# Two more and six more warm-up matmuls in the waits for the first batch's input

## The chip, the cores and the metric

The kernel runs on one core of one Trainium2 chip. The metric is the device time of the kernel in microseconds (us); lower is better. A core has five engines that work in parallel: PE (TensorE, matmuls; its weight loads are listed as PEld), DVE (VectorE), ACT (ScalarE), POOL (GpSimd) and SP (SyncE, here only the issuer of transfers). The "span" is the time from the first to the last instruction of a profiled execution; the measured time is mostly 2.1 us longer.

## The reference

For each of 8 batches, `x` (3008 x 256) goes through a Fourier transform along its length, a product with a complex filter, and the inverse transform. The result, 24064 tokens of width 256, goes through an MLP with 2048 hidden units.

```python
X = np.fft.rfft(x, axis=1)
F = (filt_r + 1j * filt_i)[None, :, :]
y = np.fft.irfft(X * F, n=x.shape[1], axis=1)
h = y.reshape(B * S, D) @ w_in
g = h * (1.0 / (1.0 + np.exp(-beta * h)))
out = g @ w_out
```

## The kernel before

The transforms are done as matmuls with tables of sines and cosines. Batch 0 has nothing to hide behind: the MLP can't start before it is transformed, so its first 40 us are a start-up stage. In it x arrives in chunks, PE multiplies eight "groups" of x by a table (`first1`), ACT or DVE copies each result from PSUM to SBUF (an "eviction"), PE transposes the results (`turn_a`), and `product` multiplies them by the filter on DVE. Meanwhile DVE, POOL and ACT compute the tables.

Matmuls on a tile of zeros, whose result nobody reads, fill PE's waits in order to keep its clock up:

```python
    def warm(n, cols=512):
        for _ in range(n):
            nc.tensor.matmul(pw[0][:, :cols], lhsT=wz[:, :P], rhs=wz[:, :cols], start=True, stop=True)
    ...
    X_FIRST = [(0, 80, 0, JG), (80, NP, 0, JG), (0, 80, JG, 2 * JG), (80, NP, JG, J)]   # the x chunks, in order
    X_FIRST += [(0, 80, g * JG, (g + 1) * JG) for g in range(2, NJG)]
    ...
    nc.sync.dma_start(mark[:], x_cur[:1, JG, :])     # SP's later filter loads wait for the third chunk
    ...
    warm(12)
    ...
    angles(0, nc.vector)      # half of the angles of table t2 on DVE
    angles(1, gp)             # the other half on POOL
    ...
    for i in range(2):
        first1(i, (True, True))                      # evictions: True is ACT, False is DVE
        warm(2)
    t2_part(0, 0)
    first1(2, (False, False))
    warm(2)
    for part in (1, 2):
        t2_part(0, part)
    for go in load_filter(fri, filt_i, M, *FG[2], nc.scalar):
        go()
    for i in range(3, 5):
        first1(i, (False, False))
        warm(2)
    t2_more(0, nc.vector)                            # three copies inside table t2, on DVE
    first1(5, (True, True))
    warm(2)
    first1(6, (True, True))
    warm(2)
    first1(7, (False, True))
    ...
    # product(i): reads the filter tile fri
        for dst, ps in zip((p_t, q_t), pss):
            nc.vector.tensor_tensor(dst[:], ps[:], fri[:, 2 * i : 2 * i + 2, :], ALU.mult)
    ...
    nc.vector.tensor_scalar_mul(t3[M:P], t3b[M:P], -1.0)   # the negation, at the start of the MLP
```

The first filter part is issued by POOL, behind x, on the software queue (q0). The other parts are issued by SP (queue q1) and ACT (q10), which are hardware queues.

## Time and profile before

Three runs: 790.11, 790.13 and 791.49 us, median 790.13 us.

| What | Before |
|---|---|
| PE busy over the span | 98% |
| Longest PE wait in start-up | 2.28 us, ending at 10.21 us |
| PE clock at half | from 11.6 to 15.0 us |
| First transpose of batch 0 (PE) | 17.09 us |
| First product of batch 0 (DVE) | 19.70 us |
| First MLP matmul (PE) | 41.36 us |

The page of the kernel before says what bounds the whole: busy time by engine, and the chain of waits by line. Lines 826 and 791 are the two MLP matmuls.

```profile
PE 772.1 (98%) x6001; PEld 548.0 (69%) x6097; DVE 395.7 (50%) x643; ACT 596.9 (75%) x920; POOL 144.6 (18%) x143
...
PE 92%; DVE 3%; issue 2%; POOL 2%; ACT 1%; DVEq 0%; ACTq 0%; POOLq 0%
```

The MLP can't be moved by a few warm-ups. Only an earlier start of it can count. PE's timeline of the kernel before shows the start-up. The columns are start, duration, engine, source line, operation, output and input, count, and in brackets the idle time before it with what ended that. `pw` is a warm-up, `psa` a group of x, `pb` the first transposes.

```profile
1.18 4.53 PE L186 MATMUL pw<-wz 128*128 128x512 bf16 x12 [1.18 <-DVE wz L181]
6.22 0.50 PE L347 MATMUL psa<-t1b,xg 94*128 94x96 bf16 x8 [0.51 <-DMA xg<-in_x_dram]
...
7.33 0.60 PE L186 MATMUL pw<-wz 128*128 128x512 bf16 x2
10.21 0.50 PE L347 MATMUL psa<-t1b,xg 94*128 94x96 bf16 x8 [2.28 <-DMA xg<-in_x_dram]
...
12.53 1.05 PE L186 MATMUL pw<-wz 128*128 128x512 bf16 x2
13.38 0.84 PE L347 MATMUL psa<-t1b,xg 94*128 94x96 bf16 x8
...
15.73 0.51 PE L347 MATMUL psa<-t1b,xg 94*128 94x96 bf16 x8
17.09 0.83 PE L409 MATMUL pb<-ident,a_t 128*128 128x128 bf16 x12 [0.86 <-POOL tiny L308]
```

The wait of 2.28 us is what the change aims at. Later a pair of warm-ups takes 1.05 us instead of 0.60, and a group 0.84 instead of 0.50. The table of windows of the same kernel shows the cause. Its columns are the stretch, its length, PE's busy time and instructions, the granted clock (1.00 is full), the DMA engines' busy share, and GB/s.

```profile
11.50:12.00 0.50, 0.46 (x3) 0.62 1.19 307
12.00:13.00 1.00, 1.00 (x11) 0.50 0.97 228
...
15.00:16.00 1.00, 1.00 (x18) 0.98 1.45 335
```

The clock is at half for 3.4 us. But is PE what the next stage waits for? The timeline of DVE and POOL in the same trace says otherwise. Lines 289 to 291 are the three table copies, 269 and 270 POOL's angle operations, the last `a_t<-psa` is the eviction that the first transpose needs.

```profile
10.58 2.89 DVE L107 CAST a_t<-psa 128x384 bf16<-128x384 f32 x6 [1.75 <-PE psa L347]
11.61 2.81 POOL L269 TENSOR_SCALAR r<-u 128x768 f32<-128x768 f32 x1
13.38 0.35 DVE L289 TENSOR_SCALAR t<-t 128x768 bf16<-128x768 bf16 x1
13.65 0.98 DVE L290 COPY t<-t 128x768 bf16<-128x768 bf16 x1
14.50 1.81 POOL L270 TENSOR_TENSOR u<-u,r 128x768 f32<-128x768 f32 x1
14.55 1.97 DVE L291 COPY t<-t 128x768 bf16<-128x768 bf16 x1
16.45 0.54 DVE L107 CAST a_t<-psa 128x384 bf16<-128x384 f32 x1
...
19.70 0.69 DVE L442 TENSOR_TENSOR pb_t<-ps,fri 128x512 bf16<-128x512 f32 x1 [1.52 <-DMA fri<-in_filt_i_dram]
```

The second copy ends at 14.63 us, just after POOL's line 269 (14.42 us); the third ends at 16.52 us, just after line 270 (16.31 us). Only then does DVE evict, and the transpose follows at 17.09 us. The label "POOL tiny" on that transpose is an inference of the profile; the eviction that ended at 16.99 us fits better. The first product then waits 1.52 us for its filter.

### The profile page before, as it was taken

To read this page: it belongs to the slowest core of one execution; us is meant where nothing else is said; L and a number is where in the kernel's file an instruction comes from. 1 tells how busy PE (TensorE), PEld (TensorE's weight loads), DVE (VectorE), ACT (ScalarE), POOL (GpSimd) and SP (SyncE) were. 2 spreads that over 40 slices of the span, in tenths; PEclk is the share of its full clock that TensorE was granted. 3 is DMA by queue.
4 is the path that set the end of the run, shared out by engine and by line. 5 is a ranking of instruction groups with operands and counts; after the bars stand their busy time and mean duration, and the time that the engine had idled before them with its cause. 6 is when DMAs were issued, how large, how long until landed. Compare 5 with 4: busy or idle time off the path is not lost.

```text
span 790.8 us, 15274 instructions
## 1 busy us (share of the span) xinstructions
PE 772.1 (98%) x6001; PEld 548.0 (69%) x6097; DVE 395.7 (50%) x643; ACT 596.9 (75%) x920; POOL 144.6 (18%) x143
## 2 busy tenths in 40 slices
PE   7899999999999999999999999999999999999998
PEld 4767667766677667776668766687667766776665
DVE  7946935755527464465634746367462760500101
ACT  5887886886678866788667876778767788677776
POOL 8421510430014200131002310024100340000000
PEclk9999999999999999999999999999999999999999
DMA  8978678116811178011860229402370214010101
GB/s 183 235 191 215 145 207 224 56 67 187 204 56 47 68 200 218 29 68 60 216 190 28 78 103 197 155 30 92 126 208 27 74 68 127 28 54 27 55 27 53
DMA packets 83379, 91.43 MB, mean 116 GB/s; under 512 B 3758, under 2 KB 73536, under 8 KB 82286
## 3 DMA queue, kind: packets, MB, share of 16 engines
q1 hardware_dynamic: 79756, 73.16, 30.0%
q0 software_dynamic: 2816, 16.26, 10.8%
q10 hardware_dynamic: 736, 1.05, 0.6%
q8 instruction: 47, 0.77, 0.4%
q14 instruction: 24, 0.20, 0.1%
HBM read 57.16 MB, written 46.66 MB: 131 GB/s over the span
## 4 chain that ended last, share of the span: by engine, by line
PE 92%; DVE 3%; issue 2%; POOL 2%; ACT 1%; DVEq 0%; ACTq 0%; POOLq 0%
PE acc L826 42%; PE hps L791 37%; PE ps L599 3%; PE ps L522 3%; PE ps L621 2%; PE ps L647 2%; DVE ost L107 1%; POOL xg L116 0%; POOL r L269 0%; DVE qb_t L442 0%; ACT a L105 0%; DVE pb_t L442 0%; PE pb L409 0%; PE psz L452 0%; DVE q_t L636 0%
## 5 line engine op out<-in xcount | busy, mean ns | idle before, releaser
L800 ACT ACTIVATE gT<-hps,beta_sb 128x512 bf16<-128x512 f32 x752 | 516.5, 687 | 175.8 <-PE hps L791 147.9
L826 PE MATMUL acc<-wout_sb,gT 128*128 128x256 bf16 x3008 | 455.1, 272 | 3.8 <-ACT ost L105 0.2
L791 PE MATMUL hps<-y,win_sb 128*128 128x512 bf16 (+7 forms) x1634 | 427.4, 350 | 0.3 <-DVE y L109 0.3
L826 PEld LDWEIGHTS <-gT 128*128 128x128 bf16 x3008 | 285.4, 98 | 132.6 <-issue 4.5
L791 PEld LDWEIGHTS <-win_sb 128*128 128x128 bf16 x1728 | 164.7, 98 | 24.8 <-issue 0.7
L637 POOL TENSOR_TENSOR v_t<-p_t,q_t 128x512 bf16<-128x512 f32 x84 | 106.7, 1270 | 376.3 <-DVE q_t L636 373.7
L107 DVE COPY ost<-acc 128x512 f32<-128x512 f32 (+1 forms) x88 | 56.2, 677 | 193.6 <-PE acc L826 188.0
L107 DVE CAST a<-ps 96x512 bf16<-96x512 f32 x96 | 65.9, 687 | 85.5 <-PE ps L599 85.4
L109 DVE TENSOR_SCALAR y<-ps 128x376 bf16<-128x376 f32 (+2 forms) x120 | 64.5, 541 | 64.4 <-PE ps L522 64.2
L632 DVE TENSOR_TENSOR p_t<-ps,frr 128x512 f32<-128x512 f32 x84 | 58.1, 691 | 31.8 <-PE ps L621 29.5
L636 DVE TENSOR_TENSOR q_t<-ps,fri 64x512 f32<-64x512 f32 x84 | 58.2, 693 | 1.2
L633 DVE SCALAR_TENSOR_TENSOR q_t<-ps,fri 64x512 f32<-64x512 f32 x84 | 57.4, 684 | 1.1
L522 PEld LDWEIGHTS <-zz 96*128 96x128 bf16 x512 | 35.3, 97 | 29.0
L105 ACT ACTIVATE z<-ps 128x512 bf16<-128x512 f32 x84 | 49.5, 589 | 0.7 <-PE ps L647 0.7
L599 PE MATMUL ps<-xg,t 94*96 94x512 bf16 x112 | 41.9, 381 | 0.8
L522 PE MATMUL ps<-t,zz 96*128 96x94 bf16 x448 | 36.7, 204 | 1.1
L116 POOL DMA_DIRECT2D xg<-in_x_dram x22 | 12.1, 556 | 114.3 <-PE acc L826 97.7
L647 PE MATMUL ps<-v_t,t 128*128 128x256 bf16 x168 | 32.1, 273 | 0.4 <-DVE q_t L636 0.4
L621 PE MATMUL ps<-a,t 128*128 128x256 bf16 x168 | 32.1, 273 | 0.4
L621 PEld LDWEIGHTS <-t 128*128 128x128 bf16 x168 | 15.8, 98 | 14.6
L599 PEld LDWEIGHTS <-t 94*96 94x96 bf16 x112 | 13.8, 123 | 12.1
L647 PEld LDWEIGHTS <-t 128*128 128x128 bf16 x168 | 15.4, 98 | 8.1 <-DVE q_t L636 0.9
(118 smaller groups left out, 196.9 us busy)
## 6 DMA issues: line engine op xcount, KB each, us to landing
out_dram<-ost SPq DMA_DIRECT2D x40, 512.0 KB, 2.8
d<-a SPq DMA_DIRECT2D x28, 384.0 KB, 3.5
a<-d SPq DMA_DIRECT2D x28, 384.0 KB, 5.2
d<-z SPq DMA_DIRECT2D x28, 384.0 KB, 2.6
zz<-d SPq DMA_DIRECT2D x28, 384.0 KB, 4.4
xg<-in_x_dram POOLq DMA_DIRECT2D x6, 1280.0 KB, 10.2
frr<-in_filt_r_dram SPq DMA_DIRECT2D x12, 256.0 KB, 6.8
out_dram<-ost SPq DMA_DIRECT2D x22, 128.0 KB, 9.0
```

Of the source, the lines that this page charges most:

```text
L107: nc.vector.tensor_copy(dst, src)
L109: nc.vector.tensor_scalar_mul(dst, src, scale)
L522: nc.tensor.matmul(ps[:, e, :NP], lhsT=zz[:, jj + e, dc * P : (dc + 1) * P], rhs=tab[:], start=True, stop=True,)
L599: nc.tensor.matmul(ps[:KP], lhsT=t1[:], rhs=s["x"][:, 2 * i : 2 * i + 2, :], start=True, stop=True)
L621: nc.tensor.matmul(ps[:, e, :], lhsT=t2[:, k0 + e, 3:5, :].rearrange("p c k -> p (c k)"), rhs=s["a2"][g][:, kk + e, :], start=True, stop=True,
L632: nc.vector.tensor_tensor(p_t[:], ps[:], frr[:, ks_, :], ALU.mult)
L636: nc.vector.tensor_tensor(q_t[:M], ps[M:P], fri[M:P, ks_, :], ALU.mult)
L637: nc.gpsimd.tensor_tensor(v_t[:], p_t[:], q_t[:], ALU.add)
L647: nc.tensor.matmul(ps[:, e, :], lhsT=t3[:, k0 + e, :], rhs=v_t[:, e, :], start=True, stop=True)
L791: nc.tensor.matmul(hps[:, pos - t0 : pos - t0 + ln], lhsT=win_sb[:, dc, fb * P : (fb + 1) * P], rhs=ys[b][:, dc, n0 : n0 + ln], start=(dc ...
L800: nc.scalar.activation(gT[:, :tn], hps[:, :tn], ACT.Silu, scale=beta_sb[:, fb : fb + 1])
L826: nc.tensor.matmul(acc[tb // per][:, tb % per, :], lhsT=gT[:, tb * P : (tb + 1) * P], rhs=wout_sb[:, fb, :], start=(fb == 0 and tb % per = ...
```

## The change

The intent is that PE is never idle for more than a microsecond in the two waits for x, so that the clock does not drop.

```diff
-    warm(12)
+    warm(14)
...
     for i in range(2):
         first1(i, (True, True))
-        warm(2)
+        warm(2 if i == 0 else 8)
     t2_part(0, 0)
```

## The prediction

> **What bounds the kernel now.** From about 41 us on, TensorE: 98% busy over the span, and the chain of waits puts 92% on PE, nearly all in the two MLP matmul lines at a granted clock of 1.00. The change touches only the first 17 us.
>
> **What the change aims at.** In PE's timeline the 12 warm-up matmuls run from 1.18 to 5.71 us; the first x chunk starts at 6.22 us (idle 0.51). After the second group's two warm-ups (7.33 to 7.93 us) PE is idle for 2.28 us until the next x transfer lands (10.21 us). The table of windows shows what follows: clock 1.00 until 11.6 us, 0.50 to about 15.0 us, then 1.00. That stretch of 3.4 us agrees with the window of 3413 ns in the Trainium skill, "TensorE: Matmul & The Clock Gate", Part 1: a window with too much idle halves the clock. In it a warm-up pair takes 1.05 us instead of 0.60, eight 94x96 matmuls 0.84 instead of 0.50.
>
> **Cost.** Warm-ups issue every 0.43 us cold (spacing of their weight loads), 0.22 us warm. Added: 2 in the first wait (0.4 to 0.85 us; the wait holds 0.5) and 6 in the second (1.3 us warm, 2.6 cold; the wait is 2.28). In the traced phase the first wait shrinks to about 0.1 us and the second to about 1.0, no x group is delayed, and I estimate that the throttle goes away. Groups 4 to 7 on PE then finish 1.5 to 2 us earlier (about 14.3 instead of 16.2 us).
>
> **How much is on the critical path: almost nothing.** Three things hide it.
> 1. The evictions of groups 2 to 4 run on DVE back to back from 10.58 to 13.47 us. Then DVE copies the twiddle table: 0.35, 0.98 and 1.97 us, though the same copies take 0.34 to 0.35 us later. They overlap GpSimd's angle operations (11.61 to 14.42, 14.50 to 16.31 us) and end just after them, as in the exclusive shared port pair of the Trainium skill, "SBUF — State Buffer", "Who interferes with whom". The last eviction of group 7 stands behind them and ends at 16.99 us; the first transpose starts at 17.09 us. Neither GpSimd nor DVE waits for PE here.
> 2. Even that start has about 1 us of slack: the first product's PSUM is complete at about 18.62 us, but DVE begins at 19.70 us, idle 1.52 us for the filter transfer, with the DMA engines about full since 4 us.
> 3. From 19.70 to 37.2 us DVE is practically full; only then come the last transposes and the MLP.
>
> So PE finishes the first stage earlier and waits longer for the same events. The gain is 0 in the traced phase; at most some tenths, perhaps 1 us, in runs where the slow stretch overlaps 17 to 20 us. The opposite phase (clock released late, added matmuls cold) delays groups 0 to 2 by 1 to 2 us, also mostly hidden.
>
> **Prediction:** 790.1 us, range 789.3 to 791.3. Faster by over 2%: 0.01; within 2%: 0.98; slower: 0.01.
>
> **What the profile should show.** 36 warm-up matmuls instead of 28; longest PE idle before 17 us about 1 us; the 0.50 stretch gone; group 7 done on PE near 14.3 us, yet the first transpose still at about 17.1 us; first product on DVE near 19.7 us; first MLP matmul near 41.4 us.
>
> **What would make it wrong.** The throttle survives a window about 70% busy; the long DVE copies follow PE or ACT rather than GpSimd; the filter transfer lands earlier, exposing PE; shifted work changes the interleaving later.

## More of the kernel before

One profile was given, with a span of 790.8 us. The execution that it shows took 792.89 us, 1.4 us more than the slowest of the three timed runs.

## The result

A ratio here is the mean time of one kernel's fast runs over the mean of the other's fast runs of the same rounds, so it is not quite the ratio of the medians quoted beside it.

| | Median | Range | Runs |
|---|---|---|---|
| Before (all runs by then) | 791.20 us | 790.11 to 792.99 | 6 |
| After | 791.86 us | 789.49 to 793.27 | 6 |

The ratio is 1.0004, with a 95% interval of 0.9984 to 1.0024: the same. The interval leaves room for a gain of 1.3 us as well as for a loss of 1.9 us. The forecast "within 2%" held. The time did not: 791.86 us lies above the predicted range of 789.3 to 791.3 us.

The profile after has a span of 789.3 us. PE's timeline:

```profile
1.17 4.93 PE L186 MATMUL pw<-wz 128*128 128x512 bf16 x14 [1.17 <-DVE wz L181]
6.22 0.50 PE L347 MATMUL psa<-t1b,xg 94*128 94x96 bf16 x8
...
7.33 1.89 PE L186 MATMUL pw<-wz 128*128 128x512 bf16 x8
9.55 0.50 PE L347 MATMUL psa<-t1b,xg 94*128 94x96 bf16 x8 [0.32 <-DMA xg<-in_x_dram]
...
13.42 0.50 PE L347 MATMUL psa<-t1b,xg 94*128 94x96 bf16 x8
14.45 0.84 PE L409 MATMUL pb<-ident,a_t 128*128 128x128 bf16 x12 [0.53 <-ACT a_t L105]
```

The warm-ups are there, the waits are short, and the table of windows of the kernel after shows the full clock throughout:

```profile
11.50:12.00 0.50, 0.50 (x9) 1.00 1.16 275
12.00:13.00 1.00, 1.00 (x20) 1.00 0.89 208
```

But x also landed earlier, at 9.55 instead of 10.21 us. The change issues no transfer, so this needs another explanation. DVE and POOL in the trace after:

```profile
9.91 2.88 DVE L107 CAST a_t<-psa 128x384 bf16<-128x384 f32 x6 [1.09 <-PE psa L347]
11.59 2.81 POOL L269 TENSOR_SCALAR r<-u 128x768 f32<-128x768 f32 x1
12.71 0.35 DVE L289 TENSOR_SCALAR t<-t 128x768 bf16<-128x768 bf16 x1
12.98 0.35 DVE L290 COPY t<-t 128x768 bf16<-128x768 bf16 x1
13.25 0.35 DVE L291 COPY t<-t 128x768 bf16<-128x768 bf16 x1
13.79 0.56 DVE L107 CAST a_t<-psa 128x384 bf16<-128x384 f32 x1 [0.20 <-PE psa L347]
...
16.23 0.69 DVE L442 TENSOR_TENSOR pb_t<-ps,fri 128x512 bf16<-128x512 f32 x1 [0.68 <-PE ps2q L433]
```

The evictions start 0.67 us earlier, because x did. The copies then start at 12.71 us and take 0.35 us each: the collision with POOL is gone. The first transpose comes 2.64 us earlier, the first product 3.47 us earlier and without a wait for the filter, and the first MLP matmul at 38.80 us, 2.56 us earlier. At the end 1.5 us is left of that (where the rest went is said under c4). The prediction's own list of what would make it wrong had this case: "the filter transfer lands earlier, exposing PE". Read alone, this pair of traces would say that the change gains 1.5 us and that the prediction's "almost nothing is on the critical path" was false. The timed runs do not show such a gain. So the questions for the experiments were whether the earlier start belongs to the change or to the run, and what makes runs of one kernel differ by several us.

### The profile page after: what moved, and what is told of

It reads as the page before. It is cut to its first block, busy times and chain, and to the rows that moved or that the text cites. A ratio compares the mean times of both kernels' runs of the same rounds, so it can differ in the third digit from the quotient of the medians.

```text
span 789.3 us, 15386 instructions
## 1 busy us (share of the span) xinstructions
PE 777.0 (98%) x6105; PEld 547.9 (69%) x6105; DVE 394.4 (50%) x643; ACT 596.8 (76%) x920; POOL 144.5 (18%) x143
## 3 DMA queue, kind: packets, MB, share of 16 engines
q0 software_dynamic: 2816, 16.26, 10.8%
q10 hardware_dynamic: 736, 1.05, 0.5%
## 4 chain that ended last, share of the span: by engine, by line
PE 91%; DMA 4%; DVE 3%; issue 1%; ACT 1%; POOL 0%; SPq 0%; DVEq 0%; POOLq 0%; ACTq 0%
PE acc L826 40%; PE hps L791 39%; PE ps L599 3%; PE ps L522 2%; PE ps L621 2%; PE ps L647 2%; DMA d<-a 1%; DMA fri<-in_filt_i_dram 1%; DVE ost L107 1%; DMA xg<-in_x_dram 1%; DMA a<-d 0%; PE psz L452 0%; DVE t L572 0%; DVE q_t L636 0%; DVE p_t L632 0%
## 5 line engine op out<-in xcount | busy, mean ns | idle before, releaser
L791 PE MATMUL hps<-y,win_sb 128*128 128x512 bf16 (+7 forms) x1728 | 447.7, 351 | 0.3 <-DVE y L109 0.3
L621 PEld LDWEIGHTS <-t 128*128 128x128 bf16 x168 | 15.9, 98 | 14.8 <-issue 0.2
```

The costliest lines, as they stand in the source:

```text
L621: nc.tensor.matmul(ps[:, e, :], lhsT=t2[:, k0 + e, 3:5, :].rearrange("p c k -> p (c k)"), rhs=s["a2"][g][:, kk + e, :], start=True, stop=True,
L791: nc.tensor.matmul(hps[:, pos - t0 : pos - t0 + ln], lhsT=win_sb[:, dc, fb * P : (fb + 1) * P], rhs=ys[b][:, dc, n0 : n0 + ln], start=(dc ...
```

## The experiments

Two theories stood at first. **Noise of the run:** transfers land at different times from run to run, and the difference between the two traces has nothing to do with the change. **Rival, a real gain:** the clock was the cause, and the gain is hidden by noise in the timed runs. The marks of all traces are collected here; "copies" are the durations of the three table copies, times are in us.

| Trace | Clock at half | Group 2 | Copies | First transpose | First product | First MLP matmul | Span |
|---|---|---|---|---|---|---|---|
| before | 11.6 to 15.0 | 10.21 | 0.35, 0.98, 1.97 | 17.09 | 19.70 | 41.36 | 790.8 |
| after | none | 9.55 | 0.35 each | 14.45 | 16.23 | 38.80 | 789.3 |
| a1, before again | none | 9.42 | 0.35 each | 14.32 | 16.06 | 38.94 | 788.1 |
| a2, after again | none | 9.54 | 0.35 each | 14.44 | 16.11 | 38.70 | 788.4 |
| a3, only the 8 | 24.0 to 27.4 | 9.66 | 0.35 each | 14.95 | 17.65 | 40.89 | 790.6 |
| a4, only the 14 | none | 9.41 | 0.35 each | 14.32 | 15.89 | 38.05 | 788.4 |
| b1, no filter wait, before | 11.6 to 15.0 | 10.26 | 0.35, 0.97, 1.98 | 17.23 | 18.79 | 40.64 | 791.3 |
| b2, no filter wait, after | none | 9.92 | 0.35 each | 14.83 | 16.40 | 38.27 | 788.0 |
| b3, no warm-ups | start to about 17.5 | 9.32 | 0.35 each | 14.09 | 16.63 | 39.03 | 789.6 |
| c1, late copies | 16.9 to 20.4 | 9.42 | 0.30, 0.97, 1.97 | 17.09 | 19.63 | 41.92 | 791.1 |
| c2, late x | none | 10.87 | 0.60, 1.97, 0.35 | 17.36 | 18.93 | 40.79 | 790.0 |
| c3, late x, 18 warm-ups | 17.9 to 21.3 | 11.24 | 0.35, 1.96, 0.35 | 17.47 | 19.66 | 42.35 | 791.9 |
| c4, early negation | 10.8 to 14.3 | 9.84 | 0.35, 0.98, 1.98 | 17.11 | 18.66 | 40.53 | 789.8 |
| d1, copies first | 25.9 to 29.3 | 10.37 | 0.35 each | 15.37 | 19.49 | 42.87 | 792.0 |
| d2, copies first, late x | 11.4 to 14.8 | 11.19 | 0.66, 1.98, 0.35 | 18.34 | 20.20 | 42.07 | 791.2 |
| d3, copies first, early negation | none | 9.40 | 1.00, 0.35, 0.35 | 14.72 | 16.58 | 38.76 | 788.5 |
| d4, as d3 with the change | none | 10.36 | 0.35 each | 15.27 | 19.47 | 41.50 | 790.7 |
| e1, both gates away | none | 9.55 | 0.69, 0.35, 0.34 | 14.86 | 16.73 | 38.70 | 788.9 |
| e2, gated queues | none | 9.96 | 0.45, 0.35, 0.35 | 14.91 | 16.47 | 39.93 | 789.1 |
| e3, gated queues with the change | none | 10.32 | 0.35 each | 15.38 | 16.95 | 40.41 | 789.6 |

From DVE's first eviction of MLP output (60 to 64 us) to the end, 18 of these 20 traces take 727.97 to 728.21 us. The other two are c3 (728.4 us) and b3 (729.1 us). So nearly all that differs between profiled runs arises in the first 64 us. "Group 2" is when PE starts it, which in most traces is when its x has landed. In b2 and c3 the warm-ups ahead of it kept PE busy until then, so there x may have landed before. (Half-clock rows are from the windows table; b3's is read from matmul durations, see there.)

### a1, a2: both kernels once more, unchanged

> The kernel before, unchanged, as a measure of the noise. If the level that I predicted from was only a lucky draw of three runs, these five lie between about 789.5 and 793.5 us with a median near 791.2, and the profile shows a first MLP matmul anywhere between 38.5 and 41.5 us, depending on when the x and filter transfers land. If the throttle alone decides (rival), every run of this kernel has a mean clock below 1.000 and the first MLP matmul is at 41 us or later in each.

> The changed kernel, unchanged. Noise theory: median 791 to 792.5 us, ratio to before within 0.2% of 1, and the first MLP matmul may land later than the 38.8 us of its first profile. Rival (the clock gain is real and carried to the end): clock 1.000 in each run, first MLP matmul again at 38.5 to 39.3 us, median at least 1.5 us under the kernel before of the same rounds.

Measured: a1 791.48 us (790.22 to 793.06, 6 runs), ratio 0.9993 (0.9971 to 1.0014); a2 791.36 us (789.68 to 793.65), ratio 0.9992 (0.9969 to 1.0014). The kernel before in the same rounds had 11 runs from 789.26 to 794.53 us, median 792.12. PE's timeline in a1, which is the kernel before:

```profile
9.42 0.50 PE L347 MATMUL psa<-t1b,xg 94*128 94x96 bf16 x8 [1.42 <-DMA xg<-in_x_dram]
...
14.32 0.85 PE L409 MATMUL pb<-ident,a_t 128*128 128x128 bf16 x12 [0.53 <-ACT a_t L105]
```

In this run of the unchanged kernel x landed at 9.4 us, PE waited only 1.42 us, the clock stayed full, and everything up to the first MLP matmul (38.94 us) came as early as in the trace after. So the 2.56 us between the first two traces are a difference between runs, not the effect of the change. The rival falls as the explanation of these two traces. The kernel before does not always lose its clock either: of the 55 runs of it that were made beside the experiments, 13 have a mean clock of 0.998 or less. (3.4 us at half clock are 0.2% of the span, so such a stretch shows as about 0.998. The drop to half after the last matmul is in the mean too, and explains some values of 0.999.)

### a3, a4: one half of the change each

```diff
-    warm(12)                    # a4 only
+    warm(14)
-        warm(2)                 # a3 only
+        warm(2 if i == 0 else 8)
```

> Only the second part: 8 warm-ups after the second group, 12 at the start. If the clock drop is caused by the 2.28 us wait, the mean clock is 1.000 as with the whole change, and groups 4 to 7 are as fast. Time: within 0.2% of before under the noise theory, about 1.5 us less under the rival.

> Only the first part: 14 at the start, 2 after the second group. The 2.28 us wait stays, so the clock should drop to 0.50 for 3.4 us as before (mean clock about 0.997) and groups 4 to 7 should be slow again. Time within 0.2% of before under both theories.

Measured: a3 793.15 us, ratio 1.0011 (0.9988 to 1.0033); a4 792.63 us, 1.0009 (0.9984 to 1.0034). Neither can be told from before. The expectations for the clock were both missed: a3 had 8 warm-ups and yet dropped to half, at 24.0 us, after waits that no warm-up of the change covers (3 of its 6 runs had a mean clock of 0.998 or less); a4 kept the 2-warm-up wait and did not drop in its profile (2 of 6 runs did). The drop is a matter of the run, in this wait and in others.

Where it falls matters too. In a3 it fell among the products, and near its end DVE waited for PE:

```profile
27.22 0.69 DVE L442 TENSOR_TENSOR pb_t<-ps,fri 128x512 bf16<-128x512 f32 x1 [0.90 <-PE ps L433]
```

PE's `ps` had just ended (26.55 us plus 0.63), so here the named releaser fits. d1's trace, at half clock from 25.9 to 29.3 us, has the same wait (0.92 us, at 29.20 us); a1's and d4's, at full clock, have none at this place. So a half clock among the products cost about 0.9 us in each of two traces. The prediction's third point ("DVE is practically full") did not hide PE there.

### b1, b2: no product waits for the filter (wrong result)

```diff
+    fz = setup.tile([P, 2, D], F32, name="fz", tag="fz")
+    nc.vector.memset(fz[:], 0.1)
...
-            nc.vector.tensor_tensor(dst[:], ps[:], fri[:, 2 * i : 2 * i + 2, :], ALU.mult)
+            nc.vector.tensor_tensor(dst[:], ps[:], fz[:], ALU.mult)
```

> The kernel before, with the first batch's products reading a constant tile instead of the filter, so that no product waits for a filter transfer (the transfers stay; the result is wrong on purpose). If late filter transfers make the spread of some 5 us between runs, the first MLP matmul comes at 37.5 to 38.5 us and the runs lie within about 2.5 us of each other, median 1 to 2 us below before. If the spread comes from elsewhere (x landing, the clock, later stages), the runs still spread over 4 us or more.

> The same constant tile in the changed kernel. If my prediction's claim is right that PE's speed before the first product is hidden, it equals the same edit of the kernel before within 0.2%. If the filter wait had been what hid a real gain of the warm-ups (rival), it is 1 to 2 us below that kernel, and its first MLP matmul is over 1 us earlier.

Measured: b1 790.61 us (789.92 to 793.10), ratio 0.9992 (0.9974 to 1.0010); b2 791.21 us (789.91 to 793.01), 0.9996 (0.9978 to 1.0014). The pair is equal within the noise, and the spread stays at about 3 us. The filter wait alone is not what spreads the runs. By luck b1's profile fell on a run like the first one: x at 10.26 us, half clock from 11.6 us, copies of 0.97 and 1.98 us, first transpose at 17.23 us. Its first product came at 18.79 us without any filter to wait for, against 16.40 us in b2. So the lateness of such a run has a cause of its own before the filter. It also means that the first MLP matmuls of b1 and b2 (40.64 and 38.27 us) can't decide between the two theories of b2's expectation: the runs differ in x.

b2 also shows the cost of the change. Its 14 warm-ups took 6.06 us, 0.43 us each, and group 0 started at 7.07 us; in the kernels with 12 warm-ups it started at 6.1 to 6.4 us. Group 2 then followed the eight warm-ups at 9.92 us without a wait. That is the "opposite phase" of the prediction.

### b3: no warm-ups at all up to the eighth group

```diff
-    warm(12)
+    warm(0)
-        warm(2)      # and so at all seven pairs
+        warm(0)
```

> The kernel before with all 28 warm-up matmuls up to the eighth group taken out, so that the clock stays at half until dense work begins. If PE's speed in this stage is hidden (my prediction), the first MLP matmul is within 0.5 us of 38.9 us and the time within 0.1% of before. If it is not hidden (rival), groups 2 to 7 take 0.84 us or more in turn, the first product starts 1 to 3 us later than 16.1 us, and the time rises by 1 to 3 us.

Measured: 793.52 us (791.75 to 794.90), ratio 1.0028 (1.0010 to 1.0047), which is slower by 0.28%. So the warm-ups that the kernel already had are worth about 2 us. But the profiled run does not show it in the place expected: PE was slow until about 17.5 us (six transposes took 0.85 us there, then 0.50), yet the first transpose came at 14.09 us, since no warm-up stood in PE's way, the first product at 16.63 us, and the first MLP matmul at 39.03 us, hardly later than a1's. This trace lost a further 1.1 us between 131 and 162 us; PE waited 0.98 us there at 133.8 us for a DMA read of batch 1's data. It is one trace, and whether the missing warm-ups caused that late read is open.

### c1: the copies start later, nothing else

In c1 two small fills delay the copies.

```diff
+    dly = setup.tile([P, 352], F32, name="dly", tag="dly")
+    for _ in range(2):
+        nc.vector.memset(dly[:], 0.0)
     t2_more(0, nc.vector)
```

> The kernel before with two DVE fills of 352 elements (estimated at about 0.7 us together, from 0.27 us for the fill of 256) ahead of the three table copies, so that they start at about 13.3 us as in the two slow profiles rather than at 12.6. If the GpSimd operations at 11.6 to 16.3 us block them when they start late, the second and third copy take about 1 and 2 us, ending within 0.3 us of a GpSimd operation's end, and the first transpose comes at about 17 us although the clock is full. If the long copies came from the slow clock of those runs (rival), they take 0.35 us each and the first transpose comes at about 15 us.

Measured: two runs, 792.66 and 793.09 us, ratio 1.0008 (0.9981 to 1.0036). The trace is what counts. DVE and POOL in c1:

```profile
11.61 2.81 POOL L269 TENSOR_SCALAR r<-u 128x768 f32<-128x768 f32 x1
12.69 0.84 DVE L375 MEMSET dly<- 128x352 f32 x2
13.45 0.30 DVE L289 TENSOR_SCALAR t<-t 128x768 bf16<-128x768 bf16 x1
13.66 0.97 DVE L290 COPY t<-t 128x768 bf16<-128x768 bf16 x1
14.51 1.80 POOL L270 TENSOR_TENSOR u<-u,r 128x768 f32<-128x768 f32 x1
14.55 1.97 DVE L291 COPY t<-t 128x768 bf16<-128x768 bf16 x1
16.44 0.55 DVE L107 CAST a_t<-psa 128x384 bf16<-128x384 f32 x1
```

And PE in c1:

```profile
17.09 1.44 PE L412 MATMUL pb<-ident,a_t 128*128 128x128 bf16 x12 [3.29 <-POOL tiny L308]
```

x landed at 9.42 us as in a1 and the clock was full, yet 0.84 us more work ahead of the copies reproduced the slow run to a few hundredths: copies of 0.97 and 1.97 us, first transpose at 17.09 us. So the collision on DVE, not the clock, makes the late first transpose: 0.84 us became 2.77 us (17.09 against 14.32). This is a cliff. Over all traces, copies that started between 13.65 and 14.7 us ended 0.2 to 0.4 us after the end of one of POOL's two operations; those from 12.55 to 13.62 us took 0.30 to 0.36 us, although POOL's line 269 was under way. Three first copies that started earlier, 0.03 to 0.59 us after that operation, were held up as well (1.00 us in d3, 0.69 in e1, 0.45 in e2): all three ended 1.03 to 1.05 us after its start. So line 269 seems to exclude the copies in about its first and its last 0.8 us, and not between. That is read off the copies; no run without POOL's operations was made.

PE's wait of 3.29 us then brought its own half clock, from 16.9 us: in this run the slow clock was a consequence of the lateness, not its cause. But it had a price: the first product waited 1.15 us for PE's `ps` and came at 19.63 us. In c4, with the first transpose at 17.11 us and the full clock after it, the product came at 18.66 us. The prediction had set this case apart ("perhaps 1 us, in runs where the slow stretch overlaps 17 to 20 us").

### c2, c3: x made late, without and with warm-ups to bridge it

```diff
-    X_FIRST = [(0, 80, 0, JG), (80, NP, 0, JG), (0, 80, JG, 2 * JG), (80, NP, JG, J)]
-    X_FIRST += [(0, 80, g * JG, (g + 1) * JG) for g in range(2, NJG)]
+    X_FIRST = [(0, 80, 0, JG), (80, NP, 0, JG), (0, 80, 2 * JG, 3 * JG), (0, 80, JG, 2 * JG), (80, NP, JG, J)]
+    X_FIRST += [(0, 80, g * JG, (g + 1) * JG) for g in range(3, NJG)]
-    nc.sync.dma_start(mark[:], x_cur[:1, JG, :])
+    nc.sync.dma_start(mark[:], x_cur[:1, 2 * JG, :])
-        warm(2)                 # c3 only
+        warm(2 if i == 0 else 18)
```

> The kernel before with a later x chunk moved ahead of the one that group 2 needs, so that the second wait grows from 1.4 or 2.3 us to about 4.5 us in every run. The clock then drops in every run (mean clock 0.998 or less), groups 3 to 7 take 0.84 us or more each for some 3.4 us, and the time rises by 2 to 6 us.

> The same with 18 warm-ups instead of 2 in that wait. If removing the throttle is worth nothing because DVE, GpSimd and the filter set the pace (my prediction), it equals the run without them within 0.1% and the first MLP matmul within 0.5 us. If the throttle is what costs (rival), the clock is 1.000, the first MLP matmul comes 1.5 to 4 us earlier and the time falls by as much.

Measured: c2 793.51 us, ratio 1.0021 (1.0002 to 1.0040), mean clock 0.998 or less in 4 of 6 runs; c3 793.78 us, ratio 1.0024 (1.0006 to 1.0042), 2 of 6 runs. A late x costs about 0.2%. Warm-ups in the wait give nothing back that these runs can show. That agrees with the prediction's core claim: in both traces the copies collide, and the first transpose comes at 17.36 and 17.47 us. It is no clean test of it, though. The 18 warm-ups filled the whole wait (group 2 at 11.24 us, without a wait, against 10.87 us in c2), c2's trace kept its clock, and c3's had a half clock of its own from 17.9 us. Its first MLP matmul came 1.56 us after c2's, where 0.5 us was expected. c2's expectation was missed in three points. The wait in its profile was 2.96 us, not 4.5, the time rose by about 1.5 us, not 2 to 6, and the clock did not drop in every run. In that very trace it did not drop after 2.96 us of idling, while in c4 it dropped after a wait of 1.89 us.

### c4: the negation moved ahead

The traces showed a second collision of the same kind. The negation of `t3` at the start of the MLP took 1.08 to 2.60 us; where it was held up it ended about 0.82 us after POOL's weight scaling (for example at 41.40 us after 40.58 us, in the trace after).

```diff
             inverse3(i - FLAG)
+    nc.vector.tensor_scalar_mul(t3[M:P], t3b[M:P], -1.0)
 ...
-    nc.vector.tensor_scalar_mul(t3[M:P], t3b[M:P], -1.0)
```

> The kernel before with the 3072-column negation of the table t3 moved from the start of the MLP to just after the last product, where DVE idles 1.6 us. So far it took 1.08 to 2.60 us and always ended about 0.82 us after a GpSimd weight scaling. If that collision is a loss of its own, the negation takes about 1.1 us, PE no longer waits for DVE's evictions near 42 us, and from the first MLP matmul to the end it takes 749.0 us or less (so far 749.2 to 750.7). Time 0.5 to 1.3 us below before, which may stay inside the noise.

Measured: 790.81 us (790.02 to 792.62), ratio 0.9984 (0.9966 to 1.0003). The negation took 0.96 us. DVE in the trace after shows the collision that c4 avoids (first fence), and c4 its new place (second fence):

```profile
39.15 2.25 DVE L572 TENSOR_SCALAR t<-t3b 64x3072 bf16<-64x3072 bf16 x1
```

```profile
36.44 0.96 DVE L497 TENSOR_SCALAR t<-t3b 64x3072 bf16<-64x3072 bf16 x1
```

The traces show what the collision costs. In nine traces with the negation in its old place and longer than 1.3 us, the stretch from the first MLP matmul to DVE's first eviction of MLP output is 20.04 us plus the negation (22.29 us with 2.25 us in the trace after, 21.40 with 1.36 in the trace before). In the six where it took 0.96 to 1.08 us the stretch is 21.15 or 21.16 us, and so it is in c4. This is a third gate, and it took back 0.9 of the 2.6 us by which the MLP started earlier in the trace after.

From the first MLP matmul to the end c4's trace took 749.27 us, which misses the expected 749.0 us; traces of the kernels that kept the negation in place took 749.1 to 750.7 us. The new place is not always clear either: in d3 the negation started at 34.47 us, inside another of POOL's scalings, and took 2.16 us. c4's interval includes 1, and d3, which contains the same edit, came out at 1.0002. So it is not shown to be faster.

### d1 to d4: the copies issued one group earlier

```diff
-    for i in range(3, 5):
-        first1(i, (False, False))
-        warm(2)
-    t2_more(0, nc.vector)
+    first1(3, (False, False))
+    warm(2)
+    t2_more(0, nc.vector)
+    first1(4, (False, False))
+    warm(2)
```

I call the collision of the copies the first gate and the wait for the filter the second. d2 adds c2's late x, d3 adds c4's early negation, d4 is d3 with the 14 and 8 warm-ups of the change.

> The kernel before with the three table copies issued before group 4 instead of after it, so that they start near 11.8 to 12.7 us, before the GpSimd operation that ends at 14.4 us can hold them up. If the cliff makes the spread, the copies take 0.35 us each whatever x does, the first transpose comes at 14.4 to 15.5 us, and six runs lie within about 2.5 us of each other, median about 1 us below before. If the spread has another cause (rival), they spread over 4 us as before.

> The same with the late x chunk of the earlier run (there the first transpose came at 17.4 us, the first MLP matmul at 40.8 us, median 793.5 us). If the copies' collision was what the late x cost, the first transpose now comes at 15.5 to 16.2 us and the time is 1 to 2 us lower. If x itself or the clock cost it (rival), it stays near 793.5 us.

> Copies one group earlier and the negation moved ahead, on the kernel before: first MLP matmul at 38 to 39.5 us, from there to the end 749.3 us or less, median 1 to 2 us below before (about 0.998).

> The same with the warm-ups of the change. If they are worth nothing here, it equals the run without them within 0.1%; if the clock drop costs once the cliff is gone (rival), it is 0.5 to 1.5 us lower and no run has a mean clock of 0.998 or less.

Measured: d1 791.37 us (789.87 to 794.18), ratio 0.9996 (0.9980 to 1.0013); d2 793.31 us, 1.0018 (1.0005 to 1.0031); d3 791.70 us, 1.0002 (0.9984 to 1.0019); d4 791.85 us, 1.0004 (0.9989 to 1.0018).

d1 and d4 were profiled in runs with a late x (10.37 and 10.36 us). The copies took 0.35 us each and the first transpose came at 15.3 us instead of 17.1: the first gate was gone. Yet DVE in d4 waited for something else:

```profile
19.47 0.69 DVE L443 TENSOR_TENSOR pb_t<-ps,fri 128x512 bf16<-128x512 f32 x1 [3.04 <-PE ps L434]
```

The named releaser had been done by about 17 us, so it was not PE; the other input is the filter tile. The queue view of what moved from 16 to 18 us supports that. Its columns are packets, MB, and the share of the DMA engines. First the kernel before, in the first trace, with x late:

```profile
q10 hardware_dynamic: 68, 0.24, 56.0%
q1 hardware_dynamic: 75, 0.11, 27.2%
q0 software_dynamic: 10, 0.02, 6.4%
```

Then a1, the same kernel with x early:

```profile
q10 hardware_dynamic: 49, 0.38, 78.3%
q1 hardware_dynamic: 50, 0.14, 30.4%
```

In the late run the software queue, which carries x and the first filter part, still has 0.02 MB to move; in a1 it is empty. In late runs its last packets trickle out until 18 to 20 us. Why is not shown: the hardware queues begin before q0 is done in both runs, and in a1 even earlier (from 13 to 14 us q1 takes 28.3% of the engines' time, against 6.5% in the first trace). In d4, whose clock was full and whose PE never waited over 1 us for x, the first product came at 19.47 us, as in the first trace. That is the prediction's second gate.

The expected gains were all missed; that d4 would equal d3 was right (1.0004 and 1.0002). Removing the first gate did not narrow the spread (d1: 4.3 us) and did not lower the median. d2 does not test its question, because its profiled run had its copies start at 13.96 us and collide all the same.

### e1 to e3: both gates away

e1 joins d1 with b1's constant tile. Its output is wrong, which doesn't matter for the time. e2 is correct: d3, with the hardware queues started later. e3 is e2 with the change's warm-ups.

```diff
-    nc.sync.dma_start(mark[:], x_cur[:1, JG, :])
+    nc.sync.dma_start(mark[:], x_cur[:1, 3 * JG, :])
-    for go in load_filter(fri, filt_i, M, *FG[2], nc.scalar):    # moved behind first1(7)
-        go()
     ...
     first1(7, (False, True))
+    for go in load_filter(fri, filt_i, M, *FG[2], nc.scalar):
+        go()
```

> Copies one group earlier and the first batch's products on a constant tile (wrong result on purpose): both gates gone. If the two gates make the spread, the first product starts at 16.0 to 17.3 us whatever the x landing, and the six runs lie within 2.5 us, at 788 to 790.5 us of span. If the spread has another cause (rival), they lie 4 us or more apart.

> A correct kernel: copies one group earlier, negation moved ahead, the SP filter transfers held until the last x chunk has landed and those of ACT issued after the eighth group. If the straggling of the first filter transfer is the second gate, the software queue is done by 15.5 us, the first product starts at 16.0 to 17.3 us, and the median is 1 to 2 us below before. If the later transfers then land too late, DVE waits for the filter at its fourth product and the gain is lost.

> The same with the change's 14 and 8 warm-ups. If the warm-ups are worth nothing even with both gates gone, it equals e2 within 0.1%. If the gates were what hid their worth (rival), it is 0.5 to 1.5 us faster than e2.

Measured: e1 790.91 us (789.63 to 792.63, a spread of 3.0 us), ratio 0.9993 (0.9976 to 1.0010); e2 791.24 us (791.04 to 793.63), ratio 1.0005 (0.9989 to 1.0022); e3 792.30 us (791.04 to 792.71, 5 runs), ratio 1.0008 (0.9992 to 1.0023).

In e3 x landed as late as in d4 (10.32 us), but the first product came at 16.95 us instead of 19.47. In e2 and e3 q0 moved nothing from 15.5 to 22 us. So holding the hardware queues back removed the second gate in these two traces. The time does not follow. In e2 the products last from 16.47 to 35.81 us, 19.3 us, where d3 needed 17.9 us (16.58 to 34.44), and DVE waits once more at 19.17 us, after the first products. That is the loss that the expectation allowed for, though the label of that wait does not prove which transfer it was. e1's spread is a little below that of the kernel before (3.2 us in the same rounds) and not below the 2.5 us expected. Its slowest run has a mean clock of 0.997; the other five lie within 1.4 us. With six runs that is a hint, not a proof. And e3 is no faster than e2: the warm-ups are worth nothing that shows even here.

No version beats both kernels beyond the noise.

## Why the prediction was right or wrong

**The step that failed is its last: "790.1 us, range 789.3 to 791.3".** A forecast of a time is the level of the kernel before plus the effect of the change, and it is the level that was mis-sized. It took the level from the median of three runs and the width from their spread of 1.4 us. The 55 runs of the kernel before that were made beside the experiments have a median of 791.89 us and go from 789.26 to 794.53 us. With a1's six they are 61: only 3 of them lie below the 790.13 us that I took as the level, the middle 80% go from 790.32 to 793.37 us, and 24 lie in my range. The 12 runs of the kernel after have a median of 791.66 us. The miss of 1.76 us (791.86 minus 790.1) is as large as the error of the level (791.89 minus 790.13); the effect of the change itself, forecast as nearly nothing, is -0.2 us between these two medians and cannot be told from zero. The profiled execution, at 792.89 us, already lay outside the range. The experiments ran on five chips, but the chip is not the cause of the spread: the medians of the kernel before were 791.21 to 792.24 us on the five, while on one of them alone its runs went from 789.26 to 794.53 us.

**What was right.**

- *"From about 41 us on, TensorE."* From 60 to 64 us to the end 18 of 20 traces agree within 0.25 us. Before that the negation on DVE decides over up to 1.5 us (see c4), so this holds from there on only.
- *The mechanism on the clock.* In the trace after, the wait was 0.32 us and the half-clock stretch was gone.
- *"Neither GpSimd nor DVE waits for PE here."* c1 showed it at full clock: the copies' collision alone put the first transpose at 17.09 us. c2 and c3 agree, in that bridging a late x with warm-ups gave nothing that could be measured. It holds up to the first transpose; after it, a half clock did make DVE wait for PE (c1, c3, a3, d1).
- *The filter as a second gate.* With x late and the first gate taken away (d1, d4), the first product still came at 19.5 us. It is real in such runs.
- *The "opposite phase"*, but smaller than forecast ("delays groups 0 to 2 by 1 to 2 us"). b2's group 0 came about 0.8 us late, and its group 2, at 9.92 us, right behind the warm-ups.

**What was wrong in the marks.** I wrote that the transpose would stay at 17.1 us, the product at 19.7 us and the MLP at 41.4 us. They came at 14.45, 16.23 and 38.80 us. The copies were expected to follow POOL, and they did; but I took their start, the landing of x and that of the filter as constants of the kernel. They were properties of one run. In a1 the unchanged kernel has the same early marks. In the one trace that I had, x landed at 10.21 us; in seven of the eleven traces up to c4 that issue x in its old order, group 2 starts at 9.66 us or earlier.

**What stays open.** Why x lands up to a microsecond later in some runs, and the first filter part with it. How much of the spread of the timed runs comes from the two gates: the traces show what they do, but the kernels without them spread nearly as much. The 13 runs of the kernel before with a low mean clock have spans that are 1.6 us longer on average than the other 42 (790.9 against 789.3 us), but c1 shows that a late run can cause the low clock, so the 1.6 us can't be put down to the clock. Part of it may be its price: about 0.9 us in a3 and d1. And whether the change makes clock drops rarer: with the full change 3 of 29 runs (after, a2, b2, d4, e3) had a mean clock of 0.998 or less. Of the 61 runs of the kernel before, 14 had. The first group are different kernels in part, and the runs are too few.

One thing I overlooked is open too. In the six kernels with the eight warm-ups (after, a2, a3, b2, d4, e3) the time exceeds the span by more than 2.25 us, by up to 3.44 us, in 11 of 35 runs. In the 129 runs of all the other kernels it never exceeds it by more than 2.20 us, c3 with its 18 warm-ups included. So something in these kernels costs time outside the span, and their profiles, which show the span alone, can look better than their times. What it is, no run shows.

## What to carry to other kernels

Before forecasting to within a few tenths of a per cent, profile and time the unchanged kernel again: here three runs within 1.4 us came from a spread of 5 us, and a trace's landing times are not constants. When a stage waits on several things, ask of each engine's speed-up which wait ends last, and then test it with a delay put in on purpose, as c1 does with a fill of 0.84 us. Two engines that exclude each other can turn a delay of tenths into microseconds, as in c1. Moving an operation clear of the other removed such a wait in the traces of d1 and c4, but the timed runs show no gain from it.

## What the Trainium skill lacked or had wrong

- "TensorE: Matmul & The Clock Gate", the table "Why this matters for your kernels", says to have no PE-idle gaps over about 3 us, and Part 1 that the cold state comes after at least one idle window of about 3.4 us. Here a gap of 1.89 us (c4) and one of 2.28 us (before) were followed by a half clock, and one of 2.96 us (c2) was not. In the 3.41 us ahead of the drop PE had been busy for 1.35 us (before) and 1.52 us (c4), so the stretch was far from idle; in c2 it was busy for 0.45 us from 7.50 to 10.91 us, and no drop followed. The length of the half-clock stretch, 3.4 us, does agree with the page.
- "SBUF — State Buffer", "Who interferes with whom", says that the shared port pair is held for a whole instruction and that the other side fully blocks. The long copies agree: they end about 0.2 us after POOL's operation (c1: 14.63 against 14.42 us). But copies that started at 12.6 to 13.6 us ran in 0.35 us while POOL's operation of 11.6 to 14.4 us was under way in the trace, and three that started in its first 0.6 us ended 1.03 to 1.05 us after its start (d3, e1, e2). By these traces it does not hold DVE up for its whole span; where it holds the port is inferred from the copies.
- No page that I drew on has it that the landing times of one program's first transfers vary from run to run: group 2's x at 9.32 to 10.37 us in kernels that issue it alike, and a last 0.02 MB of the software queue that in some runs takes until 18 to 20 us (before, d4).
